# Shorter VectorE program, swapped result queues and other load sizes in a decode kernel bound by its weight stream

## Chip, cores and metric

One core of one Trainium2 chip. The metric is the device time of one execution in microseconds, median of several executions. Where two kernels are compared, a ratio is the mean time of one kernel's fast runs over that of the other's fast runs of the same rounds, so it is not quite the ratio of the medians quoted beside it.

## The reference

One token of a transformer layer: a layer norm, attention over the last 4096 positions of a cache (32 query heads, 4 key heads), and, beside it, an MLP on a second layer norm. The output is x + attention + MLP.

```python
xn = layernorm(x)                                   # x: (1, 1, 1024), bf16
q = xn @ wq                                         # wq: 1024 x 4096
p = softmax(q . k[:, :, Sk-4096:, :] * 128**-0.5)   # 4 key heads, each used by 8 query heads
attn = (p @ v[:, :, Sk-4096:, :]) @ wo              # wo: 4096 x 1024
mlp = gelu(layernorm(xn) @ w1 + b1) @ w2 + b2       # w1: 1024 x 3584, w2: 3584 x 1024
out = x + attn + mlp
```

wq, w1, w2, wo, K and V are read once each: 39.85 MB for one token.

## The kernel before

All weights are loaded through one queue (SyncE's) in a fixed order, in pieces of whole rows. TensorE waits for each piece on its own semaphore.

```python
WQ_CHUNKS = [1, 3, 2, 2]
W1_CHUNKS = [4, 2, 2]
W2_CHUNKS = [14, 14]
WO_CHUNKS = [13, 9, 4, 2, 2, 1, 1]
...
# many small tiles first: identb, identf, onesf, ..., XNT, XNTb, ..., YTb, ...
KV = sb("KV", [128, HKV * W + HKV * NBLK * DH], dt.bfloat16)
KT = KV[:, 0:HKV * W]
WOX = KV[:, 0:4 * D]               # the last 4 rows of wo, in the space of K
W1 = sb("W1", [128, KC * F], dt.bfloat16)     # later: wo rows 0 to 27
WA = sb("WA", [128, KC * NQ], dt.bfloat16)    # wq, later w2
```

Order of the loads: wq, two heads of K, w1, two heads of K, V, then (when q is done) w2, then (when h is done) wo, its last rows when the scores are done.

The layer norm runs on VectorE in small dependent operations. A sum over partitions is a matmul with a matrix of ones:

```python
def moments(ms, T16):
    dve.tensor_reduce(out=ms[:, 0:2], in_=PS[...16 sums...])
    dve.tensor_scalar(out=ms[:, 2:4], in0=ms[:, 0:2], scalar1=INV_D, op0=mult)
    ...                                     # variance, square root on ScalarE, reciprocal
...
moments(msx, XT16)
dve.tensor_scalar(out=XNT, in0=XT16[:, 0:8], scalar1=msx[:, 2:3], scalar2=msx[:, 7:8], ...)
dve.tensor_copy(XNTb, XNT)                        # to bf16
d_xz = dve.tensor_copy(XZ[:, 96:9 * 97 - 1:97], XNTb)   # spread for the q matmuls
...                                                # the same for y, then YZ
```

The end: one pair of matmuls per wo row into two accumulators; VectorE and ScalarE each copy one half, and two queues write the halves out.

```python
d_out = DVE.mark(dve.tensor_copy(OUT[32:33, :], ACC[1]))
a_out = ACT.mark(act.activation(out=OUT[0:1, :], in_=ACC[0], func=ACTF.Copy))
act.wait_ge(ACT.sem, a_out)
act.dma_start(out_row[:, 0:512], OUT[0:1, :]).then_inc(s_out[0], 16)
sp.wait_ge(DVE.sem, d_out)
sp.dma_start(out_row[:, 512:1024], OUT[32:33, :]).then_inc(s_out[1], 16)
act.wait_ge(s_out[0], 16)
sp.wait_ge(s_out[1], 16)
```

## Time and profile before

| | before |
|---|---|
| time, median of 3 runs | 99.29 us (99.22 to 99.30) |
| span of the profiled run | 98.1 us |
| weight stream | 39.85 MB, 95.8% of the span |
| last weights landed | 95.72 us |
| last matmul ended | 96.14 us |
| last result landed | 98.10 us |

The queue lines of the page are: queue, kind, packets, MB, share of 16 engines' span.

```profile
q8 instruction: 1, 0.02, 0.1%
q10 hardware_dynamic: 34, 0.01, 0.1%
q14 instruction: 1, 0.01, 0.0%
```

Two packets inside the span are of the kind "instruction" on the page and not of the load queue's. The trace's packet records place the one of queue 14 (8192 bytes) at 77.9 us, in the middle of the stream, and the one of queue 8 (16384 bytes) at 96.8 us, after it.

### The profile page before, as it was taken

How to read it: one execution, taken by the hardware profiler on the slowest of the kernel's cores; microseconds unless marked ns; L12 is line 12 of the kernel's file. 1: busy time of each engine (PE TensorE's matmuls, PEld its weight loads, DVE VectorE, ACT ScalarE, POOL GpSimd, SP SyncE). 2: the span in 40 equal slices, each digit the busy share in tenths (PEclk: the TensorE clock that was granted, in tenths of full speed). 3: DMA queues.
4: the chain of work that ended last, by engine and by line, in shares of the span. 5: the costliest groups of instructions: out<-in, count | busy, mean ns of one | idle time of the engine just before them, and what ended most of it. 6: DMA issues, size and time to landing. Idle time of an engine off the chain costs nothing.

```text
span 98.1 us, 1063 instructions
## 1 busy us (share of the span) xinstructions
PE 68.3 (70%) x330; PEld 32.2 (33%) x330; DVE 37.1 (38%) x57; ACT 5.8 (6%) x11; POOL 6.7 (7%) x19
## 2 busy tenths in 40 slices
PE   0002199999992039999999743199991999854991
PEld 0002154555541025666644311033330334211320
DVE  4308562000008999600999544971007000000002
ACT  0500060000002000000000004000000000000002
POOL 6893000000000000000000000000000000000000
PEclk9999999999999555999999999755899579998599
DMA  5999899999998999999999999889989898999950
GB/s 170 447 453 473 379 427 427 427 397 427 449 538 374 386 409 427 456 385 427 427 427 427 427 481 503 374 386 538 386 386 523 361 488 356 436 405 413 412 215 8
DMA packets 3494, 39.89 MB, mean 406 GB/s; under 512 B 402, under 2 KB 420, under 8 KB 932
## 3 DMA queue, kind: packets, MB, share of 16 engines
q1 hardware_dynamic: 3458, 39.85, 95.8%
q8 instruction: 1, 0.02, 0.1%
q10 hardware_dynamic: 34, 0.01, 0.1%
q14 instruction: 1, 0.01, 0.0%
HBM read 39.86 MB, written 0.00 MB: 406 GB/s over the span
## 4 chain that ended last, share of the span: by engine, by line
DMA 81%; DVE 10%; SPq 4%; PE 2%; issue 1%
DMA KV<-in_A_k_cache_dram 43%; DMA KV<-in_A_wo_dram 38%; DVE KV L345 9%; PE PS L406 2%; SPq L176 1%; SPq L160 1%; SPq L166 1%; SPq L427 1%; DVE KV L568 1%; PE PS L558 0%
## 5 line engine op out<-in xcount | busy, mean ns | idle before, releaser
L345 DVE STREAM_TRANSPOSE KV<-KV 128x4096 bf16<-128x4096 bf16 x4 | 17.5, 4424 | 5.8 <-DMA KV<-in_A_k_cache_dram 5.8
L336 PE MATMUL PS<-WA,PT 128*97 x64 | 16.9, 433 | 0.1
L389 PE MATMUL PS<-W,YZ 128*97 x64 | 13.8, 380 | 4.0 <-POOLq L248 4.0
L389 PEld LDWEIGHTS PS<-W,YZ 128*97 x64 | 8.6, 134 | 9.2 <-issue 5.6
L336 PEld LDWEIGHTS PS<-WA,PT 128*97 x64 | 9.1, 142 | 7.6 <-issue 3.0
L549 PE MATMUL PS<-W,OP 128*1 128x512 bf16 x56 | 8.1, 452 | 2.8 <-DMA W<-in_A_wo_dram 2.8
L505 PE MATMUL PS<-KV,PT 128*32 128x512 bf16 x32 | 9.9, 484 | 0.1
L568 DVE CAST KV<-PS 1x512 bf16<-1x512 f32 x1 | 0.7, 683 | 19.9 <-PE PS L558 19.9
L538 PE MATMUL PS<-WA,GT 128*1 128x512 bf16 x56 | 7.9, 451 | 0.0
L406 PE MATMUL PS<-KV,LQ 128*128 x32 | 7.2, 380 | 0.5 <-DVE KV L345 0.5
L286 PE MATMUL PS<-XT,onesf 128*128 128x16 f32 x2 | 0.6, 386 | 8.7 <-DVE XT L282 8.7
L348 DVE STREAM_TRANSPOSE TT<-PS 128x1024 f32<-128x1024 f32 x1 | 1.3, 1251 | 14.1 <-PE PS L336 14.1
L505 PEld LDWEIGHTS PS<-KV,PT 128*32 128x32 bf16 x32 | 3.7, 117 | 5.9 <-issue 4.0
L549 PEld LDWEIGHTS PS<-W,OP 128*1 128x1 bf16 x56 | 2.7, 96 | 8.1 <-issue 3.2
L406 PEld LDWEIGHTS PS<-KV,LQ 128*128 x32 | 3.1, 98 | 4.6 <-issue 1.6
L538 PEld LDWEIGHTS PS<-WA,GT 128*1 128x1 bf16 x56 | 2.7, 96 | 4.7 <-issue 2.5
L510 DVE TENSOR_TENSOR TT<-PS,RM 32x512 f32<-32x512 f32 x1 | 0.7, 679 | 7.2 <-PE PS L505 7.2
L286 PEld LDWEIGHTS PS<-XT,onesf 128*128 128x128 f32 x2 | 0.5, 313 | 8.7 <-DVE XT L282 8.7
L452 ACT ACTIVATE Pe<-PS,NMB 128x512 bf16<-128x512 f32 x2 | 1.3, 684 | 28.3 <-DVE NMB L449 28.3
L570 ACT ACTIVATE KV<-PS 1x512 bf16<-1x512 f32 x1 | 0.6, 587 | 30.7 <-PE PS L558 30.7
L312 PE MATMUL PS<-YT,onesf 128*128 128x16 f32 x2 | 0.6, 384 | 2.4 <-DVE YT L309 2.4
L277 DVE STREAM_TRANSPOSE XTT<-XR 128x256 bf16<-128x256 bf16 x1 | 0.6, 630 | 4.4 <-DMA XR<-in_A_x_dram 4.4
(92 smaller groups left out, 33.7 us busy)
## 6 DMA issues: line engine op xcount, KB each, us to landing
WA<-in_B_w_dram SPq DMA_DIRECT2D x2, 3584.0 KB, 40.5
WA<-in_A_wq_dram SPq DMA_DIRECT2D x2, 2048.0 KB, 18.1
KV<-in_A_k_cache_dram SPq DMA_DIRECT2D x4, 1024.0 KB, 32.9
KV<-in_A_v_cache_dram SPq DMA_DIRECT2D x4, 1024.0 KB, 37.0
W<-in_B_w_dram SPq DMA_DIRECT2D x1, 3584.0 KB, 32.4
W<-in_B_w_dram SPq DMA_DIRECT2D x2, 1792.0 KB, 38.0
W<-in_A_wo_dram SPq DMA_DIRECT2D x1, 3328.0 KB, 34.5
WA<-in_A_wq_dram SPq DMA_DIRECT2D x1, 3072.0 KB, 11.6
```

Of the source, the lines that this page charges most:

```text
L160: sp.dma_start(WA[:, a:b], wq_pm[:, a:b]).then_inc(s_wq[j], 16)
L286: pe_sum1 = PE.mark(pe.matmul(PS[:, 7 * 512: 7 * 512 + 16], lhsT=onesf[:, :], rhs=XT16[:, 0:16]))
L336: last = pe.matmul(PS[0:97, n * 512:(n + 1) * 512], lhsT=shifted(XZ, s)[:, bass.ds(k, 1), :], rhs=wq_rows[:, bass.ds(k, 1), s * 1024 + n * ...
L345: dve.transpose(out=KT[:, g * W:(g + 1) * W], in_=KT[:, g * W:(g + 1) * W]).then_inc(r_k, 1)
L348: DVE.mark(dve.transpose(out=TT[:, :], in_=PS[:, 0:1024]))
L389: last = pe.matmul(PS[0:97, (2 + n) * 512:(2 + n) * 512 + HW], lhsT=shifted(YZ, s)[:, bass.ds(k, 1), :], rhs=w1_rows[:, bass.ds(k, 1), c: ...
L406: last = pe.matmul(PS[:, (4 + n) * 512:(5 + n) * 512], lhsT=q_blocks[:, bass.ds(g, 1), j, :], rhs=k_blocks[:, bass.ds(g, 1), n, :, j, :], ...
L452: a_exp = ACT.mark(act.activation(out=Pe[:, n * 512:(n + 1) * 512], in_=PS[:, (4 + n) * 512:(5 + n) * 512], func=ACTF.Exp, scale=SCALE, bi ...
L505: last = pe.matmul(PS[0:32, 0:512].rearrange("p (g d) -> p g d", g=HKV), lhsT=PT[:, b * 32:(b + 1) * 32], rhs=Vb[:, b, :, :], start=(b == ...
L538: pe.matmul(ACC[n], lhsT=GT[:, c:c + 1], rhs=W2[:, c * D + n * 512: c * D + (n + 1) * 512], start=False, stop=False)
L549: pe.matmul(ACC[n], lhsT=OP[:, r:r + 1], rhs=wo_at(r, 1)[:, n * 512:(n + 1) * 512], start=False, stop=False)
L568: d_out = DVE.mark(dve.tensor_copy(OUT[32:33, :], ACC[1]))
```

## The change

The intent is to shorten the VectorE program, to let the queue that looked quicker (1.12 us from issue to landing on ScalarE's, 1.20 on SyncE's, in the trace before) send the later half of the result, and to use fewer, larger loads of wo, the last 8 of its 32 rows in K's space.

```diff
-WQ_CHUNKS = [1, 3, 2, 2]
-W1_CHUNKS = [4, 2, 2]
+WQ_CHUNKS = [1, 3, 4]
+W1_CHUNKS = [2, 2, 2, 2]
-WO_CHUNKS = [13, 9, 4, 2, 2, 1, 1]
+WO_CHUNKS = [15, 9, 5, 2, 1]
+WO_IN_W1 = sum(WO_CHUNKS[:2])
...
-    identb = sb("identb", [128, 128], dt.bfloat16)
-    onesf = sb("onesf", [128, 128], dt.float32)
+    meanf = sb("meanf", [128, 128], dt.float32)      # 1/D: the scale goes into the matmul
-    XNT, XNTb, YTb = ...                             # three small tiles
+    XNTb = XZ[:, 96:9 * 97 - 1:97]                   # written in place
+    YTb = YZ[:, 96:9 * 97 - 1:97]
...
-    DVE.mark(dve.memset(PS[:, 0:4 * 512], 0.0))
+    d_ps = DVE.mark(dve.memset(PS[:, 0:6 * 512], 0.0))
...                                  # QMASK and SEL2 are now made on GpSimd
-        DVE.mark(dve.tensor_scalar(out=ms[:, 2:4], in0=ms[:, 0:2], scalar1=INV_D, ...))
...
-    DVE.mark(dve.tensor_scalar(out=XNT[:, :], ...))
-    d_xn = DVE.mark(dve.tensor_copy(XNTb[:, :], XNT[:, :]))
-    d_xz = DVE.mark(dve.tensor_copy(XZ[:, 96:9 * 97 - 1:97], XNTb[:, :]))
+    d_xz = DVE.mark(dve.tensor_scalar(out=XNTb, ...))
...
-    d_yz = DVE.mark(dve.tensor_copy(YZ[:, 96:9 * 97 - 1:97], YTb[:, :]))
-    d_zs = DVE.mark(dve.memset(PS[:, 4 * 512:6 * 512], 0.0))
...
-    act.wait_ge(ACT.sem, a_out)
-    act.dma_start(out_row[:, 0:512], OUT[0:1, :]).then_inc(s_out[0], 16)
-    sp.wait_ge(DVE.sem, d_out)
-    sp.dma_start(out_row[:, 512:1024], OUT[32:33, :]).then_inc(s_out[1], 16)
+    sp.wait_ge(ACT.sem, a_out)
+    sp.dma_start(out_row[:, 0:512], OUT[0:1, :]).then_inc(s_out[0], 16)
+    act.wait_ge(DVE.sem, d_out)
+    act.dma_start(out_row[:, 512:1024], OUT[32:33, :]).then_inc(s_out[1], 16)
```

More of the change, by code (lines that the diff above doesn't have):

```diff
@@ L104, in bass_parallel_sum__sliding_block_cached__mixer_channel_mlp__decode_kernel @@
     msx = sb("msx", [128, 8], dt.float32)
-    XNT = sb("XNT", [128, 8], dt.float32)
-    XNTb = sb("XNTb", [128, 8], dt.bfloat16)
     YT16 = sb("YT16", [128, 16], dt.float32)
@@ L109, in bass_parallel_sum__sliding_block_cached__mixer_channel_mlp__decode_kernel @@
     EXPW = sb("EXPW", [128, 1], dt.float32)
-    YTb = sb("YTb", [128, 8], dt.bfloat16)
     TT = sb("TT", [128, 1024], dt.float32)
@@ L135, in bass_parallel_sum__sliding_block_cached__mixer_channel_mlp__decode_kernel @@
     KT = KV[:, 0:HKV * W]
-    WOX = KV[:, 0:4 * D]
-    OUT = KV[0:33, 4 * D:4 * D + 512]
+    WOX = KV[:, 0:(32 - WO_IN_W1) * D]
+    OUT = KV[0:33, 12 * D:12 * D + 512]
     V = KV[:, HKV * W: HKV * W + HKV * NBLK * DH]
@@ L210, in bass_parallel_sum__sliding_block_cached__mixer_channel_mlp__decode_kernel @@
         base=0, channel_multiplier=1))
-    c_onesf = POOL.mark(pool.memset(onesf[:, :], 1.0))
-    POOL.mark(pool.memset(identb[:, :], 0.0))
+    c_meanf = POOL.mark(pool.memset(meanf[:, :], INV_D))
+    POOL.mark(pool.memset(QMASK[:, :], 1.0))
     pool.wait_ge(POOL.sem, POOL.cnt)
-    c_identb = POOL.mark(pool.affine_select(
-        out=identb[:, :], in_=identb[:, :],
-        pattern=[[-1, 128]], compare_op=ALU.not_equal, fill=1.0,
+    POOL.mark(pool.affine_select(
+        out=QMASK[:, :], in_=QMASK[:, :], pattern=[[-32, 4]], compare_op=ALU.is_ge, fill=0.0,
         base=0, channel_multiplier=1))
+    pool.wait_ge(POOL.sem, POOL.cnt)
+    c_qmask = POOL.mark(pool.affine_select(
+        out=QMASK[:, :], in_=QMASK[:, :], pattern=[[32, 4]], compare_op=ALU.is_ge, fill=0.0,
+        base=31, channel_multiplier=-1))
     POOL.mark(pool.memset(SEL[:, :], 0.0))
@@ L239, in bass_parallel_sum__sliding_block_cached__mixer_channel_mlp__decode_kernel @@
         pattern=[[-16, 2], [-1, 97]], compare_op=ALU.not_equal, fill=1.0, base=0, channel_multiplier=16))
+    POOL.mark(pool.memset(SEL2[:, :], 0.0))
+    for o in (0, 2):
+        pool.wait_ge(POOL.sem, POOL.cnt)
+        c_sel2 = POOL.mark(pool.affine_select(
+            out=SEL2[:, :], in_=SEL2[:, :], pattern=[[-1, 2]], compare_op=ALU.not_equal, fill=1.0,
+            base=-o, channel_multiplier=1))
     POOL.mark(pool.memset(XZ[:, :], 0.0))
@@ L255, in moments @@
         n = DVE.mark(dve.tensor_reduce(
-            out=ms[:, 0:2],
+            out=ms[:, 2:4],
             in_=PS[:, 7 * 512: 7 * 512 + 16].rearrange("p (a k) -> p a k", a=2),
             axis=AX.X, op=ALU.add))
-        dve_dep()
-        DVE.mark(dve.tensor_scalar(out=ms[:, 2:4], in0=ms[:, 0:2],
-                                   scalar1=INV_D, scalar2=None, op0=ALU.mult))
         dve_dep()
@@ L284, in bass_parallel_sum__sliding_block_cached__mixer_channel_mlp__decode_kernel @@
     pe.wait_ge(DVE.sem, d_xsq)
-    pe.wait_ge(POOL.sem, c_onesf)
-    pe_sum1 = PE.mark(pe.matmul(PS[:, 7 * 512: 7 * 512 + 16], lhsT=onesf[:, :], rhs=XT16[:, 0:16]))
+    pe.wait_ge(POOL.sem, c_meanf)
+    pe_sum1 = PE.mark(pe.matmul(PS[:, 7 * 512: 7 * 512 + 16], lhsT=meanf[:, :], rhs=XT16[:, 0:16]))
     dve.wait_ge(POOL.sem, c_identf)
@@ L290, in bass_parallel_sum__sliding_block_cached__mixer_channel_mlp__decode_kernel @@
     dve_dep()
-    DVE.mark(dve.tensor_reduce(out=QMASK[:, :], in_=identf[:, :].rearrange("p (t c) -> p t c", t=4),
-                               axis=AX.X, op=ALU.add))
     DVE.mark(dve.tensor_copy(REPL[:, :].rearrange("p (i c) -> p i c", i=4),
                                       SELI[:, :].unsqueeze(1).to_broadcast([128, 4, 32])))
-    dve.wait_ge(POOL.sem, c_identb)
-    DVE.mark(dve.tensor_tensor(out=SEL2[:, :], in0=identb[0:4, 0:2], in1=identb[0:4, 2:4], op=ALU.add))
     dve.wait_ge(PE.sem, pe_sum1)
     moments(msx, XT16)
-    DVE.mark(dve.tensor_scalar(out=XNT[:, :], in0=XT16[:, 0:8],
-                               scalar1=msx[:, 2:3], scalar2=msx[:, 7:8],
-                               op0=ALU.subtract, op1=ALU.mult))
+    dve.wait_ge(POOL.sem, c_lq)
+    d_xz = DVE.mark(dve.tensor_scalar(out=XNTb, in0=XT16[:, 0:8],
+                                      scalar1=msx[:, 2:3], scalar2=msx[:, 7:8],
+                                      op0=ALU.subtract, op1=ALU.mult))
     dve_dep()
-    d_xn = DVE.mark(dve.tensor_copy(XNTb[:, :], XNT[:, :]))
-    dve_dep()
-    dve.wait_ge(POOL.sem, c_z)
-    d_xz = DVE.mark(dve.tensor_copy(XZ[:, 96:9 * 97 - 1:97], XNTb[:, :]))
-    DVE.mark(dve.tensor_copy(YT16[:, 0:8], XNTb[:, :]))
+    DVE.mark(dve.tensor_copy(YT16[:, 0:8], XNTb))
     dve_dep()
@@ L311, in bass_parallel_sum__sliding_block_cached__mixer_channel_mlp__decode_kernel @@
     pe.wait_ge(DVE.sem, d_ysq)
-    pe_sum2 = PE.mark(pe.matmul(PS[:, 7 * 512: 7 * 512 + 16], lhsT=onesf[:, :], rhs=YT16[:, 0:16]))
+    pe_sum2 = PE.mark(pe.matmul(PS[:, 7 * 512: 7 * 512 + 16], lhsT=meanf[:, :], rhs=YT16[:, 0:16]))
     dve.wait_ge(PE.sem, pe_sum2)
@@ L316, in bass_parallel_sum__sliding_block_cached__mixer_channel_mlp__decode_kernel @@
     ACT.mark(act.activation(out=EXPW[:, 0:1], in_=msy[:, 6:7], func=ACTF.Exp))
-    d_y = DVE.mark(dve.tensor_scalar(
-        out=YTb[:, :], in0=YT16[:, 0:8], scalar1=msy[:, 2:3], scalar2=msy[:, 7:8],
+    d_yz = DVE.mark(dve.tensor_scalar(
+        out=YTb, in0=YT16[:, 0:8], scalar1=msy[:, 2:3], scalar2=msy[:, 7:8],
         op0=ALU.subtract, op1=ALU.mult))
-    dve_dep()
-    d_yz = DVE.mark(dve.tensor_copy(YZ[:, 96:9 * 97 - 1:97], YTb[:, :]))
-    d_zs = DVE.mark(dve.memset(PS[:, 4 * 512:6 * 512], 0.0))
     pe.wait_ge(DVE.sem, d_xz)
@@ L357, in bass_parallel_sum__sliding_block_cached__mixer_channel_mlp__decode_kernel @@
     dve.wait_ge(PE.sem, pe_qx)
-    dve.wait_ge(POOL.sem, c_lq)
     act.wait_ge(PE.sem, pe_qx)
@@ L397, in bass_parallel_sum__sliding_block_cached__mixer_channel_mlp__decode_kernel @@
     pe.wait_ge(ACT.sem, a_lq)
-    pe.wait_ge(DVE.sem, d_zs)
     k_blocks = KT.rearrange("p (g n b j a) -> p g n b j a", g=HKV, n=2, b=16, j=4, a=32)
@@ L420, in wo_at @@
     def wo_at(r, nr):
-        return W1[:, r * D:(r + nr) * D] if r < FC else WOX[:, (r - FC) * D:(r - FC + nr) * D]
+        if r < WO_IN_W1:
+            return W1[:, r * D:(r + nr) * D]
+        return WOX[:, (r - WO_IN_W1) * D:(r - WO_IN_W1 + nr) * D]
     j0 = 0
     for j, nj in enumerate(WO_CHUNKS):
-        if j0 == FC:
+        if j0 == WO_IN_W1:
             sp.wait_ge(PE.sem, pe_sc)
@@ L446, in bass_parallel_sum__sliding_block_cached__mixer_channel_mlp__decode_kernel @@
     pe_nmb = PE.mark(pe.matmul(
-        PS[:, 7 * 512 + 128: 7 * 512 + 129], lhsT=MX4[0:1, :], rhs=onesf[0:1, 0:1]))
+        PS[:, 7 * 512 + 128: 7 * 512 + 129], lhsT=MX4[0:1, :], rhs=identf[0:1, 0:1]))
     dve.wait_ge(PE.sem, pe_nmb)
@@ L483, in bass_parallel_sum__sliding_block_cached__mixer_channel_mlp__decode_kernel @@
     pe.wait_ge(s_b2, 32)
+    pe.wait_ge(POOL.sem, c_sel2)
     pe.wait_ge(DVE.sem, d_nmb)
@@ L493, in bass_parallel_sum__sliding_block_cached__mixer_channel_mlp__decode_kernel @@
     dve_dep()
-    dve.wait_ge(POOL.sem, c_mask)
     DVE.mark(dve.tensor_scalar(out=RM[:, :], in0=MASK[:, :], scalar1=REC[:, 0:1], scalar2=None, op0=ALU.mult))
@@ L570, in bass_parallel_sum__sliding_block_cached__mixer_channel_mlp__decode_kernel @@
     a_out = ACT.mark(act.activation(out=OUT[0:1, :], in_=ACC[0], func=ACTF.Copy))
-    act.wait_ge(ACT.sem, a_out)
-    act.dma_start(out_row[:, 0:512], OUT[0:1, :]).then_inc(s_out[0], 16)
-    sp.wait_ge(DVE.sem, d_out)
-    sp.dma_start(out_row[:, 512:1024], OUT[32:33, :]).then_inc(s_out[1], 16)
-    act.wait_ge(s_out[0], 16)
-    sp.wait_ge(s_out[1], 16)
+    sp.wait_ge(ACT.sem, a_out)
+    sp.dma_start(out_row[:, 0:512], OUT[0:1, :]).then_inc(s_out[0], 16)
+    act.wait_ge(DVE.sem, d_out)
+    act.dma_start(out_row[:, 512:1024], OUT[32:33, :]).then_inc(s_out[1], 16)
+    sp.wait_ge(s_out[0], 16)
+    act.wait_ge(s_out[1], 16)
     return nc
```

## The prediction

> **What bounds the kernel now.** I read the page first, then busy time by stage, then the chain of waits, then the order of events in the last 15 us.
>
> ```profile
> span 98.1 us, 1063 instructions
> ...
> PE 68.3 (70%) x330; PEld 32.2 (33%) x330; DVE 37.1 (38%) x57; ACT 5.8 (6%) x11; POOL 6.7 (7%) x19
> ...
> q1 hardware_dynamic: 3458, 39.85, 95.8%
> ...
> HBM read 39.86 MB, written 0.00 MB: 406 GB/s over the span
> ...
> DMA 81%; DVE 10%; SPq 4%; PE 2%; issue 1%
> ```
>
> No compute engine is near full; the weight queue is busy for 95.8% of the span. Busy time by stage (DMA share and GB/s are the last two columns) shows that this holds in every stage:
>
> ```profile
> 1.00:20.00 19.00, 8.73 (x26) 4.92 (x27) 7.47 (x27) 3.17 (x5) 6.33 (x14) 1.00 1.01 423
> 20.00:40.00 20.00, 14.22 (x62) 7.91 (x61) 10.18 (x6) 0.54 (x2) 0.00 (x0) 0.83 1.00 425
> 40.00:60.00 20.00, 17.52 (x86) 9.55 (x84) 11.26 (x6) 0.00 (x0) 0.00 (x0) 1.00 1.02 432
> 60.00:80.00 20.00, 14.72 (x62) 5.46 (x64) 7.39 (x18) 1.49 (x3) 0.00 (x0) 0.74 1.02 440
> 80.00:94.40 14.40, 11.64 (x94) 4.08 (x88) 0.00 (x0) 0.00 (x0) 0.00 (x0) 0.88 0.96 404
> ```
>
> From 1.0 us until the last weights the loads stream without a hole. The chain of waits says the same, because it ends in the last wo load:
>
> ```profile
> 4.69 41.86 DMA KV<-in_A_k_cache_dram
> ...
> 58.29 37.43 DMA KV<-in_A_wo_dram
> ...
> 95.76 0.40 PE PS L558 x2
> ...
> 96.19 0.68 DVE KV L568
> ```
>
> The 37.43 us is queue time and not a late issue: that load was asked for at 58.3 us, behind some 15 MB still unmoved. So time = first byte (1.0) + 39.85 MB at the stream's rate (to 95.72) + tail (2.4, to 98.1) + 1.2 outside the span (99.29 against 98.1). A part of the change counts only where it shortens one of these.
>
> In the SyncE issues, the tenth load (third K) and those after block the issuer: about nine loads are queued at once, and none of these waits leaves the DMA idle.
>
> ```profile
> 3.18 1.46 SPq L176 DMA_DIRECT2D W<-in_B_w_dram  x3
> 4.69 7.64 SPq L166 DMA_DIRECT2D KV<-in_A_k_cache_dram  x2
> 12.37 12.60 SPq L181 DMA_DIRECT2D KV<-in_A_v_cache_dram  x4
> ```
>
> [...] The trace [...] shows no loss for small loads when the queue is full: in the completion records, the last engine needs 4.26 to 4.28 us for each 1792 KB w1 load, 1.22 and 1.24 us for the 512 KB wo loads, 0.61 and 0.66 us for the 256 KB ones. Each is 25 to 27 GB/s per engine.
> [...]
> [...] operations on 1 to 8 columns take 0.16 to 0.19 us, and dependent starts are 0.20 us apart.
> [...] every change of the granted clock lies on one grid of 3.41 us (62.7, 69.5, 76.4, 79.8, 90.0, 93.4).[...]
>
> **The change part by part.**
> *VectorE.* Before the second-sum matmul (11.78 us) it loses one scale (0.20), one cast (0.21) and the copy ahead of the YT cast (0.08): 0.49 us, and perhaps 0.1 more from two small set-up operations ahead of the first moments. The q matmuls then start at about 11.9 instead of 12.49 us. The 0.91 us memset at 14.38 moves to the front: 1.76 + 0.88 (estimate from 0.91 for 1024 columns) ends near 4.1 us, and x comes at 7.65. GpSimd gains two small masks (about 0.6 each, like the one at 3.44 to 4.03) and loses an identity (0.6): its last memset ends near 8.8 instead of 8.12, before VectorE needs it at 10.4. All of this feeds q (ends 29.36), whose only effect on the stream is to release W2. Behind the loads queued at that time the stream has work until 58.8 us. Gain at the end: 0.
> *wq in 3.* Rows 5 to 8 land together at the old time, 21.9 us by the completion records, instead of 17.06 and 21.92. The matmuls on rows 1 to 4 last until about 20 to 21 us anyway (16 to 32 of them cold, 0.43 apart), and 32 warm ones at 0.216 then end at 28.8 against 29.36. Nothing.
> *w1 in 4.* Its first two rows land near 31.3 instead of 35.57, so TensorE's 4.04 us wait there goes, and h ends near 47.1 (last rows at 44.1 plus 16 x 0.19) instead of 49.6. Scores still wait for the fourth K transpose (55.35 us), so nothing is gained behind them. The 4-row load took 8.73 us against 8.54 for two of 2 rows: at most 0.19 us less stream, which I count half.
> *wo in 5.* Bytes are the same. 24 big loads become 22, so 288 of 3458 packets go, but by the equal rates above these cost next to nothing: under 0.05 us. The K space is free at 57.4 us, and the third wo load is reached by the stream near 90.8; the wait is covered by 30 us.
> *Result queues.* The ScalarE half is ready at 96.77 us and the VectorE half at 96.87. The last lines of the order of events:
>
> ```profile
> 96.18 0.59 ACT L570 ACTIVATE KV<-PS 1x512 bf16<-1x512 f32 x1 [30.67 <-PE PS L558]
> 96.19 0.68 DVE L568 CAST KV<-PS 1x512 bf16<-1x512 f32 x1 [19.89 <-PE PS L558]
> 96.80 0.25 ACTq L572 DMA_DIRECT2D out_dram<-KV  x1
> 96.90 0.32 SPq L574 DMA_DIRECT2D out_dram<-KV  x1
> ```
>
> The completion records put the landings at 97.92 (1.12 us after issue) and 98.10 (1.20). Swapped: 96.80 + 1.20 = 98.00 and 96.90 + 1.12 = 98.02. Gain 0.08 us.
> *TensorE at the end.* One row is 0.606 us of stream. Counting back from 95.72 the new wo loads land at 85.3 (15 rows), 90.8 (9), 93.8 (5), 95.1 (2) and 95.72 (1). Before:
>
> ```profile
> 84.26 2.97 PE L549 MATMUL PS<-W,OP 128*1 128x512 bf16 x26 [0.37 <-DMA W<-in_A_wo_dram]
> 89.61 5.09 PE L549 MATMUL PS<-W,OP 128*1 128x512 bf16 x30 [2.39 <-DMA W<-in_A_wo_dram]
> 94.54 0.95 PE L549 MATMUL PS<-KV,OP 128*1 128x512 bf16 x6
> 95.76 0.38 PE L558 MATMUL PS<-KV,OP 128*1 128x512 bf16 x2 [0.28 <-DMA KV<-in_A_wo_dram]
> ```
>
> A row is a pair of matmuls, 0.214 us warm and 0.427 cold. After the 2.39 us gap the old 9 rows ran cold from 90.0 to 93.4, and TensorE had just caught up when row 31 landed at 95.06. New: 15 warm pairs fill 85.4 to 88.6, then a gap of 2.15 us. Warm: 9 pairs to 92.8, 5 to 94.9, 2 to 95.5, the last at 95.76 as before. One cold window: 17 pairs from 90.8, 8 of them cold in 3.41 us and 9 warm in 1.93, end at 96.14 against 96.16 before, plus up to 0.25 for how the waits fall. Expected loss about 0.1.
> Sum: -0.09 (stream, half of 0.19) - 0.03 (packets) - 0.08 (result) + 0.10 (TensorE) = -0.10 us: 99.29 to 99.2.
>
> **The rivals.**
> 1. *TensorE becomes the bound at the tail.* For it: the larger chunks leave 17 rows for the last 4.9 us[...] (PV was cold from 63.8 to 69.5). Then 16 pairs are cold, which is 90.8 + 6.83 + 0.21 = 97.8 instead of 96.16: +1.7 us, about 100.9. Against: the gap shrinks from 2.39 to 2.15 us[...]
> 2. *The score chain gets later.* With h done at 47.1, TensorE idles between the third and the fourth K transpose (2.7 us), and the last 8 score matmuls may run cold: +1.5 us at most. W2 ended at 83.9 and the first wo load now lands 1.2 us later, at 85.3, so this is nearly covered: +0 to 0.1 us.
> 3. *Fewer loads make the stream faster*, as a fixed cost per load would have it (two fewer loads at about 0.25 to 0.5 us each): 98.3 to 98.8. Against it stand the 0.61 us of a 256 KB load, which leave no room for such a cost.
> 4. *The shorter VectorE chain is worth its 0.5 us at the end:* 98.8. The stage view speaks against it, since the stream never waits.
>
> **Range and chances.** The center is 99.2. Rivals 3 and 4 and a luckier order of the engines give 98.7 below; an unlucky clock phase and differences of the stream between runs give 99.7 above. Two per cent is 2 us, more than any single term but rival 1 at its worst can move. So: faster 0.015, same 0.97, slower 0.015.
>
> **What would show each step right or wrong.** The DMA share stays at 1.0 to 94 us, and the last wo load lets TensorE start at 95.6 to 95.8. The q matmuls start near 11.9; the w1 wait of 4.04 us is gone and h ends near 47; scores still end at 57.4 to 58.9. The wo matmuls start at 85.4, 90.8, 93.8, and the last pair at 95.7 to 96.3; later than that is rival 1. The results are issued at 96.8 by SyncE and 96.9 by ScalarE. I am wrong if the last load lands before 95.3 (the packets cost more than their rates show) or if the pair before last starts after 96.2.

The marked cuts are statements of how the hardware works that no trace of this case shows; what was measured stays. No term of the sum is cut: it came to -0.10 us, as it stands there. To read it:

- The operations on 1 to 8 columns are VectorE's. Two of them in that trace, at 10.74 and 13.65 us, took 0.29 us and not 0.16 to 0.19.
- Cold is a granted clock of 0.50 and warm one of 1.00; a window is one step of the grid of 3.41 us. In the trace before the clock was cold from 32.0 to 38.8, 62.7 to 69.5, 76.4 to 79.8 and 90.0 to 93.4 us, so twice for two windows and twice for one.
- The one cold window in the sum is my estimate from the last of these. Rival 1 counts two, 6.83 us, as at PV. That two are less likely than one was not shown.
- The 0.25 to 0.5 us per load of rival 3 is an assumption, with no measurement behind it.

## The result

99.38 us (99.36 to 99.44, 4 runs) against 99.30 us (99.22 to 99.40, 4 runs); ratio 1.0009, 95% interval 0.9992 to 1.0026. The same time.

The page of the changed kernel, same lines as before:

```profile
span 98.0 us, 1056 instructions
...
PE 69.0 (70%) x330; PEld 32.1 (33%) x330; DVE 36.6 (37%) x49; ACT 5.8 (6%) x11; POOL 7.1 (7%) x23
...
q1 hardware_dynamic: 3170, 39.85, 96.2%
q8 instruction: 1, 0.02, 0.1%
q10 hardware_dynamic: 34, 0.01, 0.1%
HBM read 39.86 MB, written 0.00 MB: 407 GB/s over the span
...
DMA 84%; PE 9%; SPq 4%; issue 1%; DVE 1%; POOLq 0%
```

VectorE shows 8 instructions less and 288 packets are gone, as intended. The line of queue 14 is gone as well: no instruction packet falls into the stream. The stream itself was not quicker by as much as this would suggest. Busy time in the same stretches (the last two columns are DMA share and GB/s), before:

```profile
24.00:74.00 50.00, 38.27 (x163) 19.15 (x161) 26.96 (x26) 2.03 (x5) 0.00 (x0) 0.86 1.02 435
...
94.40:94.80 0.40, 0.40 (x8) 0.13 (x4) 0.00 (x0) 0.00 (x0) 0.00 (x0) 1.00 0.32 118
94.80:95.20 0.40, 0.40 (x6) 0.08 (x2) 0.00 (x0) 0.00 (x0) 0.00 (x0) 1.00 0.09 36
```

and after:

```profile
24.00:74.00 50.00, 39.67 (x162) 19.39 (x161) 26.74 (x25) 2.03 (x5) 0.00 (x0) 0.83 1.01 429
...
94.40:94.80 0.40, 0.40 (x7) 0.14 (x5) 0.00 (x0) 0.00 (x0) 0.00 (x0) 1.00 0.90 338
94.80:95.20 0.40, 0.40 (x6) 0.17 (x4) 0.00 (x0) 0.00 (x0) 0.00 (x0) 1.00 0.11 36
```

Two things have changed that cancel. Here and below, an engine of the stream is one of the 16 DMA engines that share every load (each load has 16 completion records in the trace). Before, at 94.4 to 94.8 us most of them had already moved their last bytes (share 0.32), and the kernel waited for the last engine until 95.72. After, nearly all are still busy there (0.90), and then all finish together. So the stream lost its straggler (the engine that finishes well after the others) and got slower as a whole: 429 instead of 435 GB/s between 24 and 74 us. The completion records of the last wo load (one per engine) say it in two numbers: the median engine finished at 94.81 us before and 95.32 after, the last one at 95.72 and 95.49. (A completion is recorded later than the end of the data: the last packets of weights ended at 95.38 and 95.03 us.)

The end of the chain after, and TensorE's last bursts:

```profile
48.09 42.39 DMA W<-in_A_wo_dram
90.48 0.04 issue
90.52 5.30 PE PS L545 x32
95.83 0.23 PE PS L554 x2
```

```profile
85.11 3.40 PE L545 MATMUL PS<-W,OP 128*1 128x512 bf16 x30 [0.49 <-DMA W<-in_A_wo_dram]
90.52 3.71 PE L545 MATMUL PS<-W,OP 128*1 128x512 bf16 x18 [2.01 <-DMA W<-in_A_wo_dram]
94.02 1.81 PE L545 MATMUL PS<-KV,OP 128*1 128x512 bf16 x14
95.66 0.38 PE L554 MATMUL PS<-KV,OP 128*1 128x512 bf16 x2
...
96.70 0.32 SPq L568 DMA_DIRECT2D out_dram<-KV  x1
96.80 0.25 ACTq L570 DMA_DIRECT2D out_dram<-KV  x1
```

In this run TensorE was the last link from 90.5 us on: 17 pairs, one cold window from 90.9 to 94.3 (granted clock 0.50), last matmul at 96.04 us, 0.55 us after the last weights instead of 0.42. The results landed at 97.83 and 98.01 us.

The front of the program, before and then after (one line of TensorE and one of VectorE each):

```profile
8.31 0.17 DVE L280 CAST XT<-XTT 128x8 f32<-128x8 bf16 x1
...
35.88 13.75 PE L389 MATMUL PS<-W,YZ 128*97 x64 [4.04 <-POOLq L248]
```

```profile
8.03 0.76 DVE L286 CAST XT<-XTT 128x8 f32<-128x8 bf16 x1
...
31.62 7.94 PE L384 MATMUL PS<-W,YZ 128*97 x32
```

The wait of 4.04 us for w1 is gone. One 8-column cast took 0.76 us instead of 0.17 and ended with GpSimd's last memset (8.77 us), which the added masks had pushed back by 0.65 us; why the one waits for the other was not tried. It ate most of the 0.49 us that I had counted: q started at 12.21 us, against 12.49 before.

### The profile page after: what moved, and what is told of

The parts are those of the page before. It is cut to its first block, busy times and chain, and to the rows that moved or that the text cites. A ratio compares the mean times of both kernels' runs of the same rounds, so it can differ in the third digit from the quotient of the medians.

```text
span 98.0 us, 1056 instructions
## 1 busy us (share of the span) xinstructions
PE 69.0 (70%) x330; PEld 32.1 (33%) x330; DVE 36.6 (37%) x49; ACT 5.8 (6%) x11; POOL 7.1 (7%) x23
## 4 chain that ended last, share of the span: by engine, by line
DMA 84%; PE 9%; SPq 4%; issue 1%; DVE 1%; POOLq 0%
DMA W<-in_A_wo_dram 43%; DMA W<-in_B_w_dram 40%; PE PS L545 5%; PE PS L384 3%; SPq L175 1%; SPq L165 1%; SPq L159 1%; DVE KV L564 1%; SPq L423 0%; PE PS L554 0%; POOLq L257 0%
## 5 line engine op out<-in xcount | busy, mean ns | idle before, releaser
L332 PE MATMUL PS<-WA,PT 128*97 x64 | 15.9, 412 | 1.2 <-POOLq L257 1.1
L384 PE MATMUL PS<-W,YZ 128*97 x64 | 14.7, 387 | 1.4 <-POOLq L257 1.3
L332 PEld LDWEIGHTS PS<-WA,PT 128*97 x64 | 8.6, 134 | 8.1 <-issue 4.0
L400 PE MATMUL PS<-KV,LQ 128*128 x32 | 7.7, 394 | 2.4 <-DVE KV L341 2.4
L545 PE MATMUL PS<-W,OP 128*1 128x512 bf16 x48 | 7.1, 458 | 2.5 <-DMA W<-in_A_wo_dram 2.5
L292 PE MATMUL PS<-XT,meanf 128*128 128x16 f32 x2 | 0.6, 385 | 9.1 <-DVE XT L288 9.1
L545 PEld LDWEIGHTS PS<-W,OP 128*1 128x1 bf16 x48 | 2.2, 94 | 6.9 <-issue 2.6
L292 PEld LDWEIGHTS PS<-XT,meanf 128*128 128x128 f32 x2 | 0.5, 310 | 9.1 <-DVE XT L288 9.1
L202 DVE MEMSET PS<- 128x3072 f32 x1 | 2.6, 2618 | 0.6 <-issue 0.6
L427 DVE TENSOR_REDUCE MXP<-PS 128x1 f32<-128x1024 f32 x1 | 1.2, 1225 | 2.5 <-PE PS L400 2.5
```

The lines of the kernel that those rows point to most:

```text
L202: d_ps = DVE.mark(dve.memset(PS[:, 0:6 * 512], 0.0))
L332: last = pe.matmul(PS[0:97, n * 512:(n + 1) * 512], lhsT=shifted(XZ, s)[:, bass.ds(k, 1), :], rhs=wq_rows[:, bass.ds(k, 1), s * 1024 + n * ...
L384: last = pe.matmul(PS[0:97, (2 + n) * 512:(2 + n) * 512 + HW], lhsT=shifted(YZ, s)[:, bass.ds(k, 1), :], rhs=w1_rows[:, bass.ds(k, 1), c: ...
L400: last = pe.matmul(PS[:, (4 + n) * 512:(5 + n) * 512], lhsT=q_blocks[:, bass.ds(g, 1), j, :], rhs=k_blocks[:, bass.ds(g, 1), n, :, j, :], ...
L427: d_mxp = DVE.mark(dve.tensor_reduce(out=MXP[:, 0:1], in_=PS[:, 4 * 512:6 * 512], axis=AX.X, op=ALU.max))
L545: pe.matmul(ACC[n], lhsT=OP[:, r:r + 1], rhs=wo_at(r, 1)[:, n * 512:(n + 1) * 512], start=False, stop=False)
```

## Experiments

Twelve kernels, in three groups of four; each group ran on one chip beside the kernel before. All gave correct results.

### One part alone: four kernels

**a1: only the result queues swapped**, the last hunk of the change on the kernel before.

> Only the two result queues swapped. My prediction's step: 0.08 us less, because the ScalarE queue is quicker by that much. Theory S, formed from the two traces: the second result to leave lands 1.20 us after its issue whichever queue issues it, so the span stays at 98.1 us, and because the span after the change was shorter by 0.08 us but the time was not, ending on ScalarE instead of SyncE costs 0.1 us outside the span: time +0.05 to +0.15 us.

**a2: only the VectorE program** (all VectorE and GpSimd hunks, with the small tiles that go).

> Only the shorter VectorE program (with its GpSimd masks). The stream theory: q starts near 12.2 us instead of 12.49, the last weights land at the old time, time within 0.1 us of before. The rival that the chain counts at the end: 0.3 to 0.5 us less, near 98.9 us.

**a3: only wo in five loads**, with the last 8 rows in K's space.

```diff
-WO_CHUNKS = [13, 9, 4, 2, 2, 1, 1]
+WO_CHUNKS = [15, 9, 5, 2, 1]
+WO_IN_W1 = sum(WO_CHUNKS[:2])
```

> Only the five wo loads. The stream theory: last weights land within 0.1 us of before; TensorE has 17 rows left after the second load and ends between 96.1 and 96.4 us, bound by cold matmuls if a cold window falls in: time 0 to +0.2 us. The rival of a fixed cost per load: two loads fewer give 0.5 us less or more.

**a4: only wq in three loads and w1 in four.**

```diff
-WQ_CHUNKS = [1, 3, 2, 2]
-W1_CHUNKS = [4, 2, 2]
+WQ_CHUNKS = [1, 3, 4]
+W1_CHUNKS = [2, 2, 2, 2]
```

> Only wq in three loads and w1 in four. My prediction's step: stream shorter by about 0.09 us (the 4-row load took 8.73 us against 8.54 for two of two rows). Stream theory otherwise: h ends near 47.5 us, scores at most 1.5 us later, nothing at the end: time within 0.1 us of before. The rival that the score chain decides: +0.3 us or more.

Measured, beside 99.27 us for the kernel before: a1 99.50 (ratio 1.0021, 1.0007 to 1.0034), a2 99.52 (1.0022, 1.0009 to 1.0036), a3 99.32 (1.0005, 0.9991 to 1.0018), a4 99.47 (1.0023, 1.0009 to 1.0036). None is faster, and the parts add up to +0.7% where the whole change has +0.1%. So the parts do not simply add, which the stream theory (the prediction's view that the stream of loads sets the time) did not expect.

The traces of a1, a3 and a4 have the queue 14 packet, at 77.1 to 78.2 us, and a straggling engine. The trace of a2 has neither, like the changed kernel. And a2 has the slow stream of the changed kernel: its median engine finishes at 95.45 us, while those of the other three finish at 94.75 to 94.96. So both of the opposite effects come with the VectorE part.

What in a part that only shortens VectorE's program can slow a load? Its tiles. It drops identb, XNT, XNTb and YTb, 352 bytes per partition net, and all tiles declared later move down. In the compiled programs KV, W1 and WA start at bytes 38912, 104448 and 161792 before (all multiples of 512) and 352 bytes lower after, which is 160 over a multiple of 512.

I formed two theories from these numbers. Alignment: the start of the weight tiles decides how long the packets take. It is a multiple of 512 bytes in the kernels whose median engine finishes at 94.75 to 94.96 us (before, a1, a3, a4) and 160 over one where it finishes at 95.32 and 95.45 (after, a2). Refill, my name for it in b3's expectation: the instruction packet of queue 14 belongs to VectorE and goes away when its program is short. The four traces with 73 VectorE instructions have it, the two with 63 do not (counted by the size of the compiled program; the profile's 57 and 49 leave out waits and the like). Neither is shown by these traces alone. The rivals are scatter from build to build, and an instruction packet of TensorE.

### Alignment and instruction packet, each undone by itself

**b1: the changed kernel, weight tiles moved back.**

```diff
+    PAD = sb("PAD", [128, 88], dt.float32)        # 352 unused bytes per partition
     KV = sb("KV", [128, HKV * W + HKV * NBLK * DH], dt.bfloat16)
```

> The changed kernel with 352 unused bytes per partition ahead of the weight tiles, so that they start at byte 38912 again (a multiple of 512, as before) and not at 38560 (160 over one). Alignment theory: a K or V load of 8 KB packets takes 2.45 us again instead of 2.48, the median engine is 0.35 to 0.45 us earlier at the end of W2, the last weights land near 95.0 to 95.1 us; time 0.3 to 0.5 us under the changed kernel, near 98.9 to 99.0. Rival, scatter from build to build: time within 0.15 us of the changed kernel.

98.79 us (98.72 to 98.91), ratio to before 0.9945 (0.9931 to 0.9958). The changed kernel has 1.0009, so 352 unused bytes are worth 0.64% or 0.6 us. The median engine finished w2 0.33 us earlier than in the changed kernel, a little less than expected, and the last weights landed at 95.00 us.

**b2: the kernel before, weight tiles moved 160 bytes.**

```diff
+    PAD = sb("PAD", [128, 40], dt.float32)        # 160 unused bytes
     KV = sb("KV", [128, HKV * W + HKV * NBLK * DH], dt.bfloat16)
```

> The kernel before with 160 unused bytes ahead of the weight tiles, so that they start 160 bytes over a multiple of 512, as after the change. Alignment theory: K and V loads take 2.48 us, the last weights land near 96.1 us, time +0.3 to +0.5 us: 99.6 to 99.8. Scatter theory: within 0.15 us of before.

100.18 us (100.11 to 100.39), ratio 1.0089 (1.0073 to 1.0106): +0.9 us, more than I expected. The last weights landed at 96.36 us, 0.64 later than before, and the median engine finished 0.61 later. Scatter is ruled out: the two moves go in opposite directions, as the alignment theory has it, and nothing else differs.

The packet records show it packet by packet. The median packet of 8192 bytes takes 309 ns in every trace with the tiles at the old start, and 311 or 312 ns in each of the four with shifted tiles. Over all packet sizes the difference is 0 to 5 ns, and over the 176 or 192 weight packets of one engine it adds up to 0.3 to 0.4 us (an estimate from the medians by size), more than half of the 0.5 to 0.6 us by which the median engine is later.

**b3: b1 with ten more VectorE instructions**, in a place where VectorE has time to spare.

```diff
     d_GT = DVE.mark(dve.tensor_tensor(out=GT[:, :], in0=HT[:, :], in1=U2[:, :], op=ALU.mult))
+    for i in range(10):
+        dve.memset(PAD[:, i:i + 1], 0.0)
```

> The aligned changed kernel with ten more 1-column VectorE memsets far from the end path, so that VectorE's program is as long as before. Refill theory: the 8192-byte instruction packet at 77 to 78 us, seen in the four traces with the long VectorE program and in neither with the short one, is back, one engine is 0.3 to 0.6 us behind the median at the end, time +0.2 to +0.4 us over the aligned kernel. Rival, the refill belongs to TensorE or to chance: no packet there and the same time.

99.55 us (99.32 to 99.66), ratio 1.0019 (1.0004 to 1.0035): +0.75 us for ten memsets that nothing waits for, some twice what I had put down. (The profiled run of b3 was one of its faster ones: its span is 0.51 us longer than that of b1.) The queue lines of its page:

```profile
q1 hardware_dynamic: 3170, 39.85, 95.8%
q8 instruction: 1, 0.02, 0.1%
q10 hardware_dynamic: 34, 0.01, 0.1%
q14 instruction: 1, 0.01, 0.0%
```

The packet is back, at 77.1 us. Busy time in b3 just before its last weights land, then in b1:

```profile
94.40:94.80 0.40, 0.40 (x6) 0.06 (x2) 0.00 (x0) 0.00 (x0) 0.00 (x0) 1.00 0.22 82
94.80:95.20 0.40, 0.40 (x6) 0.09 (x4) 0.00 (x0) 0.00 (x0) 0.00 (x0) 1.00 0.05 20
```

```profile
94.40:94.80 0.40, 0.40 (x6) 0.09 (x4) 0.00 (x0) 0.00 (x0) 0.00 (x0) 1.00 0.24 87
94.80:95.20 0.40, 0.38 (x6) 0.08 (x2) 0.00 (x0) 0.00 (x0) 0.00 (x0) 1.00 0.00 0
```

In both most engines are done by 94.8. In b1 nothing is left after that; in b3 a little is, one engine's share, and the kernel waits for it until 95.50 us instead of 95.00.

**b4: b1 with the result queues as before.**

> The aligned changed kernel with the result queues as before. My prediction's step: 0.08 us more than the aligned kernel. Theory S: the last result lands 1.95 us after the last matmul either way, time within 0.05 us (if ending on ScalarE costs 0.1 us outside the span, 0.1 us less).

98.62 us (98.58 to 98.76), ratio 0.9927 (0.9912 to 0.9941), the fastest kernel; it beats the kernel before by 0.7% and the changed one by 0.8%. The swap costs 0.18% here, and a1 has 0.21%. Inside the span it does nothing: from the end of the last matmul to the last landing it takes 1.95 to 1.97 us in all fourteen traces, whichever queue sends which half. Outside the span (time of the profiled run less its span) the four kernels that end on ScalarE's queue have 1.39, 1.39, 1.39 and 1.42 us, the ten that end on SyncE's 1.24 to 1.35. Over all runs, b1 and b4 have the same mean span (97.37 and 97.38 us) and differ outside it (1.43 and 1.26). The queue is not the only thing that counts there, though: a2 and b2 end on SyncE's and have a mean of 1.39 and 1.38 over their five runs. This part is not in the trace, so why it is longer stays open.

### The other terms

**c1: the short VectorE program and aligned tiles, loads and queues as before** (a2 with the 352 bytes).

> The short VectorE program with the weight tiles aligned; loads and result queues as before. If the load sizes are worth nothing, as the stream theory has it, 98.5 to 98.7 us, the same as the aligned changed kernel with the old queues (98.62 on another chip visit: ratio to before 0.9927). If the changed load sizes gain (my 0.1 us, or more by a fixed cost per load), 0.1 us or more above it; if they lose, below it.

98.84 us, ratio 0.9943 (0.9930 to 0.9957). Against a2 (1.0022), the 352 bytes are worth 0.8%. Against b4, the old load sizes cost 0.16%, and against c2 (next) 0.05%: the new sizes are worth 0.05 to 0.16 us, within the intervals of these ratios.

**c2: b4 with three more memsets of 1024 columns in the chain ahead of the first moments.**

```diff
+    for _ in range(3):
+        DVE.mark(dve.memset(TT[:, :], 0.0))
+        dve_dep()
     dve.wait_ge(PE.sem, pe_sum1)
     moments(msx, XT16)
```

> The aligned changed kernel with the old queues and three memsets of 1024 columns put in the chain ahead of the first moments, some 2 to 3 us. Stream theory: q starts and ends later, the time stays within 0.1 us of 98.6. Rival, the VectorE chain counts at the end: +2 us.

98.74 us, ratio 0.9938 (0.9924 to 0.9951), so within 0.11% of b4. The memsets took 0.91 us each, and q started 3.3 us later than in the changed kernel:

```profile
15.54 16.80 PE L336 MATMUL PS<-WA,PT 128*97 x64
```

The length of VectorE's chain counts for nothing at the end here; the number of its instructions does (b3, ten more: 0.75 us).

**c3: b4 with the tiles 64 bytes further.**

```diff
-    PAD = sb("PAD", [128, 88], dt.float32)
+    PAD = sb("PAD", [128, 104], dt.float32)
```

> The same kernel with the weight tiles 64 bytes further, so a multiple of 64 but not of 128. If any start off a multiple of 256 or 512 costs the same, 99.1 to 99.5 us, as at 160 over; if 64 bytes are enough, 98.6.

99.24 us (99.13 to 99.51), ratio 0.9983 (0.9969 to 0.9996): 0.45 to 0.56% over c2 and b4. A start 64 over a multiple of 512 is not enough. Starts of 128 and 256 over a multiple of 512 were not tried.

**c4: b4 with w2 in 14 loads of two rows.**

```diff
-W2_CHUNKS = [14, 14]
+W2_CHUNKS = [2] * 14
```

> The same kernel with w2 in 14 loads of two rows instead of 2 of 14: twelve loads more. Stream theory with equal packet rates: within 0.15 us of 98.6. Rival, a fixed cost of 0.25 to 0.5 us per load: +3 to +6 us.

99.26 us, ratio 0.9989 (0.9976 to 1.0003): 0.5 to 0.6% over c2 and b4. Neither expectation holds. Twelve loads more cost 0.5 to 0.6 us, 0.04 to 0.05 us each. The completion records agree: w2 took 17.49 us on the median engine against 16.97 in b4, so 0.043 us per load. That is about a sixth of the rival's smallest fixed cost and not the nothing that I had read from the rates. The packet records give a likely source: with aligned tiles the median packet of 2048, 4096 and 8192 bytes takes 84, 159 and 309 ns, so 75 ns for every 2048 bytes and 9 ns more for the packet. A load more is 8 weight packets more for each engine (the page of c4 has 1728 packets more than that of b4, 144 a load or 9 an engine, of which one has under 512 bytes), 0.07 us by this estimate. Whether a load costs anything beyond its packets was not tried.

### All traces together

Weight tiles are "on" when they start at a multiple of 512 bytes. The straggler is how far the last engine is behind the median one at the end of the last wo load.

| kernel | VectorE instructions | tiles | queue 14 packet | median engine, us | last engine, us | straggler, us | ratio to before |
|---|---|---|---|---|---|---|---|
| before | 73 | on | 77.9 | 94.81 | 95.72 | 0.91 | 1 |
| a1 | 73 | on | 78.2 | 94.96 | 95.97 | 1.01 | 1.0021 |
| a3 | 73 | on | 77.1 | 94.75 | 95.54 | 0.79 | 1.0005 |
| a4 | 73 | on | 77.2 | 94.89 | 95.97 | 1.08 | 1.0023 |
| b3 | 73 | on | 77.1 | 94.72 | 95.50 | 0.78 | 1.0019 |
| b2 | 73 | 160 over | 77.2 | 95.42 | 96.36 | 0.94 | 1.0089 |
| after | 63 | 160 over | none | 95.32 | 95.49 | 0.17 | 1.0009 |
| a2 | 63 | 160 over | none | 95.45 | 95.76 | 0.31 | 1.0022 |
| c3 | 63 | 64 over | none | 95.28 | 95.75 | 0.47 | 0.9983 |
| b1 | 63 | on | none | 94.83 | 95.00 | 0.17 | 0.9945 |
| b4 | 63 | on | none | 94.74 | 95.09 | 0.35 | 0.9927 |
| c1 | 63 | on | none | 94.83 | 95.30 | 0.47 | 0.9943 |
| c2 | 67 | on | none | 94.75 | 95.02 | 0.27 | 0.9938 |
| c4 | 63 | on | none | 95.26 | 95.55 | 0.29 | 0.9989 |

Column by column: a packet when and only when VectorE has 73 instructions; the straggler 0.78 us or more with the packet and 0.47 or less without; the median engine at 94.72 to 94.96 with aligned tiles and at 95.28 to 95.45 without, c4 apart, which has twelve loads more. Each cell is one profiled execution, and repeats of one kernel were not profiled, so differences of 0.2 us between rows of a kind mean little.

The straggler's place in time ties it to the packet. Between the last load of w2, which lands near 75 us, and the first of wo, which lands at 83 to 85, the last engine falls further behind the median in all six traces with the packet: before from 0.49 to 1.00 us, a1 0.44 to 1.10, a3 0.24 to 0.89, a4 0.26 to 1.21, b2 0.40 to 0.97, b3 0.40 to 0.86. In the other eight it moves by 0.02 us or less. So 0.24 to 0.49 us of these six stragglers was there before the packet, and 0.46 to 0.95 us came with it. The packet itself took 0.31 to 0.33 us; why the loss is larger stays open. The ten memsets of b3 had run by 66.3 us, before any of this. The packet appears somewhere between 67 (c2) and 73 instructions; that it holds VectorE's own instructions is inferred from this, not read from the trace.

Only one layout with the weight tiles at multiples of 512 (KV at 38912) and three with them elsewhere were tried.

## Why the prediction was right, and what was wrong in it

The time was inside the range, and the ground given for "same" holds: no single term moved the 2 us that it would have taken. But that the measured +0.09% came so near the sum's -0.10 us was luck. The sum rests on parts that hardly touch the stream, and the VectorE part touched it twice, in opposite directions. Walking from before to after through kernels that differ in one thing each, in per cent of the time before: the short VectorE program with aligned tiles -0.57 (c1, with its GpSimd masks), the load sizes -0.16 (b4), the swapped queues +0.18 (b1), the shift of the tiles +0.64 (after): together +0.09. Three chip visits are in this sum, each against the kernel before, and each step has an uncertainty near 0.2.

- *Stream and tail as the bound: right.* c2 delays VectorE's chain by some 3 us and changes the time by 0.11%, within its interval. Rival 4 is dead in the form in which I wrote it.
- *"VectorE ... Gain at the end: 0": wrong, and the largest miss.* The chain is worth 0, as said, but the shorter program took the instruction packet out of the stream, worth 0.57 us (c1) to 0.75 (b1 against b3). I had the queue 14 line in front of me and passed it over, as a packet of 0.01 MB. It counts because one engine falls behind there (by 0.46 to 0.95 us in the six traces with it), and the kernel waits for the last engine (in b3 until 95.50 us, with the median at 94.72).
- *A missing term: where the weight tiles start.* It has no place in my sum. The diff shows the dropped tiles, and their sizes (320 bytes per partition, 352 with padding) are enough to see a shift that is no multiple of 512. It cost 0.6 to 0.9 us, about as much as the packet's absence gained.
- *"Packets ... under 0.05 us": a size off.* 0.043 us per load makes it 0.09 us for the two loads that go. The rates that I called equal span 25 to 27 GB/s per engine, too wide to show 9 ns a packet.
- *"Result queues ... gain 0.08 us": wrong in its step.* I took the time from issue to landing as the issuing engine's (1.12 for ScalarE, 1.20 for SyncE). It goes by order: after the swap SyncE's, now the first, took 1.13 us and ScalarE's, now the second, 1.21. The swap gained nothing from the last matmul to the last landing and cost some 0.2 us in the time (a1 0.21%, b1 against b4 0.18%).
- *w1, half of 0.19 us: not shown.* The 8.73 and 8.54 us were read from the last engine alone; on the median engine the same loads took 8.59 and 8.57, so the term had no ground. a4 was slower by 0.23%; its profiled run lost the most at the instruction packet (0.95 us), but why new load sizes should make that worse none of the runs explains. In c1 against c2, new sizes of wq, w1 and wo together are worth 0.05%.
- *TensorE at the end: right.* Predicted starts 85.4, 90.8 and 93.8 us, measured 85.1, 90.5 and 94.0; one cold window of the two that rival 1 needed, end at 96.04 against 96.14 predicted. It cost 0.13 us in that run and nothing in b1, b4 and c2, whose pages show no cold slice after 88 us. h ended at 47.7 us (47.1 predicted) and the scores at 57.7, as said.
- *Rival 2, a later score chain: came in part and cost nothing.* TensorE idled for 2.36 us before the last 8 score matmuls, which took 2.32 us instead of 1.90; the scores ended 0.3 us later than before, and the loads that they release were asked for at 57.7 us, over 30 us before the stream reached them.
- *q at 11.9 us: 12.21*; the cast took 0.59 us longer than before. It did not matter.
- *Rival 3, a fixed cost of 0.25 to 0.5 us per load: wrong* by c4, which measured 0.04 to 0.05 us for each load more.

## What to carry to other kernels

When a stream of loads is the bound, look at everything that lands on its engines and at how its packets lie: here one instruction packet of 8192 bytes came with 0.46 to 0.95 us of delay on the last engine, and the removal of small tiles, 352 bytes per partition, moved every large tile declared after them, which cost 0.64% (after against b1). Put the large tiles first or pad, and check their start bytes after any edit. A change that measures "the same" may be a gain and a loss; here one line of padding turned it into a gain of 0.55% and, with the old result queues, of 0.73%.
